# Talking-heads attention and two dense layers in float32: the first stage issued in the order of a list scheduler inside the kernel

## Chip, cores and metric

One core of a Trainium2 chip. The metric is device time in microseconds (us) of one execution, lower is better. Engines by the profile's names: PE (TensorE, matmuls), ACT (ScalarE), DVE (VectorE), POOL (GpSimd), SP (SyncE, which here only issues DMAs).

## What is computed

```python
scores = scale * np.matmul(q, k.transpose(0, 1, 3, 2))      # 4 batches, 12 heads, 448 x 448, head size 64
scores = np.einsum('bhij,hg->bgij', scores, w_pre)          # mix the heads
attn = np.exp(scores - np.max(scores, axis=-1, keepdims=True))
attn = attn / (np.sum(attn, axis=-1, keepdims=True) + 1e-09)
attn = np.einsum('bhij,hg->bgij', attn, w_post)             # mix the heads again
x = np.matmul(attn, v)                                      # as 1792 tokens x 768
x = ((x @ w1) * (x @ w2)) @ w3 @ w_out                      # 768 -> 1024 -> 1024 -> 768
out = np.maximum(np.maximum(x @ v1, x @ v2), x @ v3) @ vo   # 768 -> 768 -> 768
```

The dense weights arrive as 64-bit floats and are turned into float32 on the chip.

## The kernel before

It has two stages. In the first, the attention of all four batches runs with the dense layers of batches 0 and 1 beside it. In the second (`last_two`), the dense layers of batches 2 and 3 run together with seven instead of eight block products. The change leaves the second stage as it is.

**Attention.** A batch has 23 steps (`NP`) of 20 queries, 92 in all. *Scores* (`scores`, L208): a unit of 128 queries of a head pair (or the last 64 of two pairs) is four 64x64 matmuls at L215, one eviction (L217 or L219) and one store to `sdram`; 21 units a batch. *Regroup* (L229) loads the 20 queries back with queries and heads in the partitions, two steps ahead (`AHEAD`). *Mix and softmax* (`mix_softmax`): four matmuls at L250 into the bank pair `m`, the maximum on DVE (L252), two exponentials on ACT (L256), then the weights `kwr` on DVE. *Post* (`post_mix`), one step later: 32 small matmuls at L284 into `p`, copied to `a` on ACT (L291). After every sixth step and the last of a batch, `attend` multiplies by `v` (48 matmuls at L316), and the result goes to `xdram`. The tags `m`, `p` and `s` have one pair of PSUM banks each. A float32 matmul shows as two instructions in the trace.

**Dense work beside it.** All dense products are split in a high and a low half, three matmuls each (`products`, L120). `fuse` forms w3 @ w_out (384 matmuls of 384 columns), `moe(b)` the layers of a batch (864 of 448 columns). A weight block of first use goes through `from_f64` (POOL issues the load `wraw`, one ACT pass, four DVE passes), is split (ACT, then DVE at L164) and stored to `kept`; batch 1 reads it from there. `weight_sums` has POOL form the sums for the second stage.

**What sets the order.** The loop over steps writes a step as regroup, scores, mix, post, and then `fill`s in dense groups of six matmuls at a rate of 2.4 or 3.9 groups a step:

```python
        rate = 2.4 if s < LAG + NP else 3.9
        for third in range(3):
            fill(rate / 6)
            if third:
                some_scores(third)
            fill(rate / 6)
```

The scores of batch b+1 are spread over the steps of batch b, head pair by head pair (`ahead_scores`). The framework then orders the instructions of each engine itself from the program so written; each engine takes its own in that fixed order.

Of the kernel before, what the change touches and what calls it, by code (L numbers as in the profile page):

```python
# [17 lines left out]
P = 128  # L18
# [33 lines left out]
def units():  # L52

    for pr in range(0, HP, 2):
        for x in (pr, pr + 1):
            for it in range(S // P):
                yield [(x, P * it), (x, P * it + HB)]
        yield [(pr, S // P * P), (pr + 1, S // P * P)]
# [3 lines left out]
def attention_talking_heads_moe_kernel(  # L62
# [37 lines left out]
    def from_f64(t, src, w):  # L100
        raw = pa.tile([P, PW], I64, tag="wraw", name="wraw", bufs=3)
        nc.gpsimd.dma_start(raw[:, :w], src)
        words = raw[:, :w].bitcast(U32).rearrange("p (x two) -> p x two", two=2)
        low, high = words[:, :, 0], words[:, :, 1]
        ti = t.bitcast(U32)
        nc.scalar.activation(t, high.bitcast(F32), AF.Abs)  # L106
        nc.vector.tensor_scalar(t, t, F64_MIN, F64_MAX, op0=ALU.max, op1=ALU.min)
        nc.vector.tensor_scalar(ti, ti, 5, 2, op0=ALU.logical_shift_left, op1=ALU.logical_shift_right)
        nc.vector.scalar_tensor_tensor(ti, low, 29, ti, op0=ALU.logical_shift_right, op1=ALU.bitwise_or)  # L109
        nc.vector.scalar_tensor_tensor(ti, high, 0xC0000000, ti, op0=ALU.bitwise_and, op1=ALU.bitwise_or)  # L110

    def wc():
        return pa.tile([P, PW], F32, tag="wc", name="wc", bufs=3)

# [12 lines left out]

# [8 lines left out]
    stored = set()  # L138

    def split_f64(hi, lo, src, w):  # L140
        t = wc()[:, :w]
        from_f64(t, src, w)
        nc.scalar.copy(hi, t)
        nc.gpsimd.tensor_sub(lo, t, hi.bitcast(F32))

    def slab_tiles():
        hi = wp.tile([P, KH * P], F32R, tag="whi", name="whi")
        lo = wp.tile([P, KH * P], F32R, tag="wlo", name="wlo")
        return hi, lo

    def slab(nk, key):
        hi, lo = slab_tiles()
        hi, lo = hi[:, :nk * P], lo[:, :nk * P]
        if key in source and key not in stored:
            t = wc()
            from_f64(t, source[key], PW)
            nc.scalar.copy(hi, t)
            nc.scalar.dma_start(kept[key], t)
            stored.add(key)
        else:  # L160
            t = lo.bitcast(F32)
            nc.sync.dma_start(t, kept[key])
            nc.scalar.copy(hi, t)  # L163
        nc.vector.tensor_sub(lo, t, hi.bitcast(F32))  # L164
        return hi.rearrange("p (k f) -> p k f", f=P), lo.rearrange("p (k f) -> p k f", f=P)

    kp = const.tile([P, HB], F32, name="kp")
    kw = const.tile([P, H, GB], F32, name="kw")  # L170

# [19 lines left out]
    xst, est, ast, vst = {}, {}, {}, {}  # L191

    def load_heads():

        t = [big.tile([P, HP, S], F32, tag=x, name=n) for x, n in (("xhi", "kall"), ("xlo", "qall"))]
        for a, z in ((0, 2), (2, HP)):
            for dst, src, w in zip(t, (kT, qT), (S, P)):
                nc.sync.dma_start(dst[:, a:z, :w], src[0, a:z, :, :w].rearrange("x p j -> p x j"))
        nc.sync.dma_start(t[1][:, :, P:], qT[0, :, :, P:].rearrange("x p j -> p x j"))
        return [[x[:, pr] for x in t] for pr in range(HP)]  # L200

    def load_pair(b, pr):
        t = [pa.tile([P, S], F32, tag=x, name=x, bufs=3) for x in "kq"]
        for dst, src in zip(t, (kT, qT)):
            nc.sync.dma_start(dst, src[b, pr])
        return t

    def scores(b, unit, heads, tag="s", eng=None, out=None):  # L208
        st = out if out is not None else pa.tile([P, 2, S], F32, tag="s", name="s", bufs=2)
        pt = banks(tag)  # L210
        for c, (pr, i) in enumerate(unit):
            k, q = heads[pr]
            for o in range(2):
                sl = slice(o * D, (o + 1) * D)
                nc.tensor.matmul(pt[HB * c:HB * c + HB, o, :S], q[sl, i:i + HB], k[sl], start=True, stop=True)  # L215
        if eng is nc.vector:
            nc.vector.tensor_scalar_mul(st, pt[:, :, :S], D ** -0.5)  # L217
        else:
            nc.scalar.activation(st, pt[:, :, :S], AF.Copy, scale=D ** -0.5)  # L219
        if out is None:  # L220
            issue = nc.sync if eng is nc.vector else nc.scalar
            (pr, i), (other, _) = unit
            if other == pr:
                issue.dma_start(sdram[b][i:i + P, 2 * pr:2 * pr + 2], st)
            else:
                for c, (pr, i) in enumerate(unit):
                    issue.dma_start(sdram[b][i:i + HB, 2 * pr:2 * pr + 2], st[HB * c:HB * c + HB])

    def regroup(b, p):  # L229
        x = pa.tile([P, 2, S], F32, tag="x", name="x", bufs=AHEAD + 1)  # L230
        i = 2 * GI * p
        if i + 2 * GI <= S:
# [625 lines left out]
```

## Time and profile before

| | us |
|---|---|
| median of 3 runs | 1285.13 (1279.38 to 1285.81) |
| the profiled execution | 1290.92 |
| its span, first to last instruction | 1289.0 |
| PE busy | 1151.6 (89%) |
| DVE busy | 743.5 (58%) |
| ACT busy | 599.5 (47%) |
| POOL busy | 211.7 (16%) |
| mean granted TensorE clock | 0.948 of full |
| moved by DMA | 262.56 MB, mean 204 GB/s |

Busy time is the time in which an engine has an instruction under way. A matmul overlaps the next one, so the distance of two starts, and not the length of one, is what a matmul costs. The granted clock has two levels, 2.4 GHz (1.00) and 1.2 GHz (0.50); a mean between them says how the time was shared. All shares of the page are over both stages.

### The profile page before, as it was taken

The page shows a single profiled execution, that of the slowest core. Times are in us where ns is not written, and L with a number is a line of the kernel's source. Part 1 is how long each engine was busy: PE and PEld are TensorE (multiplying, and loading weights), DVE is VectorE, ACT ScalarE, POOL GpSimd, SP SyncE. Part 2 cuts the span into 40 slices and gives each one's busy share as a digit, 9 for nine tenths or more (in the row PEclk, how much of TensorE's full clock was granted, in tenths as well). Part 3 has the DMA queues.
Part 4 walks back from the last instruction along what each step waited for, and adds up shares of the span by engine and source line. Part 5 has one row for each costly group of instructions (what it writes and reads, how often), then busy time and mean ns, then how long its engine had stood idle before and what let it go on. Part 6 is the DMA issues. An engine that isn't in the chain of part 4 may idle for free.

```text
span 1289.0 us, 29211 instructions
## 1 busy us (share of the span) xinstructions
PE 1151.6 (89%) x12348; PEld 923.7 (72%) x12348; DVE 743.5 (58%) x1191; ACT 599.5 (47%) x1139; POOL 211.7 (16%) x245
## 2 busy tenths in 40 slices
PE   5678989997898997887998889989899999999998
PEld 1345757765576875755776677778798889988887
DVE  4764544465764477582654545454377675468784
ACT  3555665555655546563563444345343334333331
POOL 3441211000000000002356645620000000000000
PEclk8789999999998998898898889899999999999999
DMA  9987787775886587766887878662543332133334
GB/s 339 303 256 244 238 259 268 241 243 188 275 263 219 168 267 263 244 226 208 276 292 254 270 242 295 228 189 81 186 129 116 100 118 56 53 99 107 108 97 136
DMA packets 113470, 262.56 MB, mean 204 GB/s; under 512 B 23592, under 2 KB 67644, under 8 KB 113340
## 3 DMA queue, kind: packets, MB, share of 16 engines
q1 hardware_dynamic: 57180, 116.94, 29.9%
q0 software_dynamic: 15456, 77.62, 18.5%
q10 hardware_dynamic: 40704, 66.14, 14.2%
q8 instruction: 97, 1.59, 0.5%
q14 instruction: 33, 0.27, 0.1%
HBM read 176.50 MB, written 84.15 MB: 202 GB/s over the span
## 4 chain that ended last, share of the span: by engine, by line
PE 45%; DMA 16%; DVE 12%; ACT 9%; issue 3%; ACTq 0%; POOL 0%; DVEq 0%; SPq 0%; POOLq 0%
PE w L120 20%; PE p L120 5%; PE m L120 5%; PE s L120 5%; DMA xdram<-xs 3%; PE p L316 3%; PE p L284 3%; DVE wlo L164 2%; ACT e L256 2%; DMA wlo<-kept_w 2%; PE m L250 2%; DVE nmax L252 2%; DVE wc L109 2%; DMA wlo<-kept_m 2%; DMA wlo<-kept_b 1%
## 5 line engine op out<-in xcount | busy, mean ns | idle before, releaser
L256 ACT ACTIVATE e<-m,nmax 128x448 f32<-128x448 f32 (+1 forms) x184 | 114.9, 630 | 128.4 <-DVE nmax L252 104.4
L284 PEld LDWEIGHTS p<-kwr,e 60*64 60x64 f32 x5760 | 116.3, 149 | 76.9 <-issue 33.0
L252 DVE TENSOR_REDUCE nmax<-m 128x2 f32<-128x896 f32 (+1 forms) x92 | 99.8, 1085 | 73.5 <-PE m L250 73.4
L250 PE MATMUL m<-x,kp 60*64 60x448 f32 x720 | 104.8, 606 | 39.3 <-ACT e L256 39.3
L284 PE MATMUL p<-kwr,e 60*64 60x60 f32 x5760 | 119.5, 234 | 17.2 <-DVE kwr L263 13.7
L164 DVE TENSOR_TENSOR wlo<-wlo,whi 128x768 fp32r<-128x768 f32 (+1 forms) x58 | 67.6, 1166 | 112.3 <-ACT whi L163 112.2
L120 PE MATMUL w<-yhi,wlo 128*128 128x448 f32 (+1 forms) x292 | 108.2, 370 | 5.1 <-DVE wlo L164 5.1
L120 PE MATMUL w<-yhi,whi 128*128 128x448 f32 (+1 forms) x292 | 112.7, 386 | 0.0
L120 PE MATMUL w<-hhi,whi 128*128 128x448 f32 (+1 forms) x280 | 107.8, 386 | 5.3 <-ACT hhi L349 5.3
L163 ACT CAST whi<-wlo 128x768 fp32r<-128x768 f32 (+1 forms) x58 | 52.4, 903 | 124.4 <-DMA wlo<-kept_m 42.4
L120 PE MATMUL w<-ylo,whi 128*128 128x448 f32 (+1 forms) x292 | 108.1, 370 | 0.0
L120 PE MATMUL w<-hlo,whi 128*128 128x448 f32 (+1 forms) x280 | 103.6, 370 | 1.3 <-POOL hlo L350 1.3
L120 PE MATMUL w<-hhi,wlo 128*128 128x448 f32 (+1 forms) x280 | 103.1, 368 | 0.0
L215 PE MATMUL s<-k,q 64*64 64x448 f32 x504 | 66.3, 597 | 34.2 <-ACT s L219 34.2
L291 ACT COPY a<-p 128x480 f32<-128x480 f32 x180 | 93.2, 577 | 2.5 <-PE p L284 2.5
L219 ACT ACTIVATE s<-s 128x896 f32<-128x896 f32 x73 | 67.0, 918 | 55.7 <-PE s L215 23.6
L250 PEld LDWEIGHTS m<-x,kp 60*64 60x64 f32 x720 | 26.4, 142 | 82.2 <-ACT e L256 55.9
L316 PE MATMUL p<-a,v 128*64 128x120 f32 (+1 forms) x1536 | 77.3, 260 | 4.8 <-ACT a L291 4.8
L316 PEld LDWEIGHTS p<-a,v 128*64 128x64 f32 x1536 | 73.8, 137 | 10.2 <-ACT a L291 5.8
L106 ACT ACTIVATE wc<-wraw 128x768 f32<-128x768 f32 (+1 forms) x64 | 54.7, 856 | 52.7 <-DVE wlo L164 17.8
L260 DVE TENSOR_SCALAR den<-den 128x2 f32<-128x2 f32 (+1 forms) x92 | 20.8, 226 | 98.1 <-ACT e L256 98.0
L120 PE MATMUL w<-xhi,whi 128*128 128x448 f32 x192 | 75.9, 396 | 0.1
(198 smaller groups left out, 2474.2 us busy)
## 6 DMA issues: line engine op xcount, KB each, us to landing
x<-sdram SPq DMA_DIRECT2D x176, 210.0 KB, 5.5
sdram<-s ACTq DMA_DIRECT2D x62, 448.0 KB, 5.0
wraw<-in_wm POOLq DMA_DIRECT2D x18, 768.0 KB, 6.4
wlo<-kept_m SPq DMA_DIRECT2D x27, 384.0 KB, 3.1
wlo<-kept_w SPq DMA_DIRECT2D x18, 512.0 KB, 3.6
wraw<-in_w3T POOLq DMA_DIRECT2D x16, 512.0 KB, 6.1
kept_m<-wc ACTq DMA_DIRECT2D x18, 384.0 KB, 4.1
wc<-kept_m POOLq DMA_DIRECT2D x18, 384.0 KB, 6.8
```

Of the source, the lines that this page charges most:

```text
L106: nc.scalar.activation(t, high.bitcast(F32), AF.Abs)
L120: nc.tensor.matmul(out, w, r, start=(k == 0), stop=(k == 3 * n_k - 1))
L163: nc.scalar.copy(hi, t)
L164: nc.vector.tensor_sub(lo, t, hi.bitcast(F32))
L215: nc.tensor.matmul(pt[HB * c:HB * c + HB, o, :S], q[sl, i:i + HB], k[sl], start=True, stop=True)
L219: nc.scalar.activation(st, pt[:, :, :S], AF.Copy, scale=D ** -0.5)
L250: nc.tensor.matmul(pt[HB * c:HB * c + HB, u, :S], kp[sl], x[sl, c], start=True, stop=True)
L252: nc.vector.tensor_reduce(out=nmax[:r], in_=pt[:r, :, :S], axis=AX.X, op=ALU.max, negate=True)
L256: nc.scalar.activation(e[:r, u], pt[:r, u, :S], AF.Exp, bias=nmax[:r, u:u + 1], scale=1.0, accum_out=den[:r, u:u + 1])
L284: nc.tensor.matmul(pt[HB * side:HB * side + HB, c, t, :, u * GB:u * GB + m], e[sl, u, j:j + HB], kwr[sl, u, :, :m], start=True, stop=True,)
L291: nc.scalar.copy(ast[b][:, :, :, off:off + w].rearrange("p t g i -> p (t g) i"), pt[:, c, :, :, :w].rearrange("p t g i -> p (t g) i"),)
L316: nc.tensor.matmul(pt[o * D:(o + 1) * D, pr // 3, pr % 3, :], vst[b][:, jc, h * D:(h + 1) * D], a[:, jc, h, :], start=(jc == 0), stop=(jc ...
```

## The change

The first stage is no longer written in the order of its loops. Every piece of work (one unit's four matmuls, one eviction, one DMA, six dense matmuls, ...) is handed to `Plan` with an engine, a duration, a key and the tiles it reads and writes. `Plan.order` then plays the engines through in time: each takes, of what is ready, the piece with the lowest key. A DMA adds its bytes to one pipe at 0.29 MB/us, counts as landed 1.7 us after it has left the pipe, and is offered only while the pipe is less than 2.5 us behind. A piece may name two engines (evictions: ACT or DVE; a weight's low half: DVE or POOL) and goes to the first that is free. `manual_schedule` keeps the instructions in the order in which `emit` writes them.

The keys count steps. `unit` takes scores row by row: K of a whole batch stays in `kall`, Q comes in rows of 128 queries, and the 21 units of batch b+1 have keys one step apart, from 12 steps after batch b's first step on. `fuse` has the keys 6.5 to 23.8, the dense layers of batch 0 24.6 to 62, those of batch 1 from 62 on. Of batch 1, the last product (108 matmuls) is kept for after the attention (`rest_of_one`). The first row of batch 0 is stored in two parts, 40 queries of each head pair first, and the first regroups wait for that part only. `attend` is cut in two halves. Stores that ACT issued are issued by SP.

```diff
+ENGINES = ("PE", "ACT", "DVE", "POOL", "SP")
+HOP = 0.12
+SWITCH = 0.28
+LAND = 1.7
+RATE = 0.29
+FIRST = 2 * 2 * GI
+BACK = 2.5
...
+    def __call__(self, eng, took, key, do, reads=(), writes=(), bytes=0, mode=None):
+        deps = set()
...
+            while loads and pipe - now < BACK:
+                key, x = heapq.heappop(loads)
+                (e, took), = self.ops[x][0].items()
+                if busy[e]:
+                    later.append((key, x))
+                    continue
+                busy[e] = True
+                out.append((x, e, now))
+                pipe = max(pipe, now + took) + self.ops[x][4] / RATE / 1e6
+                heapq.heappush(events, (now + took, 0, x, e))
+                heapq.heappush(events, (pipe + LAND, 1, x, None))
...
+                while not busy[e] and ready[e]:
+                    _, x = heapq.heappop(ready[e])
+                    if taken[x]:
+                        continue
+                    taken[x] = True
+                    took, m = self.ops[x][0][e], self.ops[x][5]
+                    if e == "PE" and m != mode:
+                        took, mode = took + SWITCH, m
+                    busy[e] = True
+                    out.append((x, e, now))
+                    heapq.heappush(events, (now + took, 0, x, e))
+                    heapq.heappush(events, (now + took, 3, x, e))
+                    heapq.heappush(events, (now + took + HOP, 1, x, e))
...
+    def emit(self):
+        for x, e, _ in self.order():
+            self.ops[x][2](e)
...
+    kall = pa.tile([P, HP, S], F32, name="kall", bufs=1)
+    qs = ring(2, [P, HP, P], "q")
...
-    def load_pair(b, pr):
-        t = [pa.tile([P, S], F32, tag=x, name=x, bufs=3) for x in "kq"]
-        for dst, src in zip(t, (kT, qT)):
-            nc.sync.dma_start(dst, src[b, pr])
...
-        if out is None:
-            issue = nc.sync if eng is nc.vector else nc.scalar
-            (pr, i), (other, _) = unit
-            if other == pr:
-                issue.dma_start(sdram[b][i:i + P, 2 * pr:2 * pr + 2], st)
...
+        plan({"ACT": 0.95, "DVE": 1.12}, 0, key + 0.05, evict, bank_of, [where])
+        if whole and not r and not b:
+            for x, (i, z) in enumerate(((0, FIRST), (FIRST, P))):
+                dma("SP", key + 0.06 + 0.8 * x, sdram[b][i:z, 2 * u:2 * u + 2], out[i:z], 3584 * (z - i), [where],
+                    [("sd", b, r - 1 if x == 0 else r, u)])
+        elif whole:
+            dma("SP", key + 0.06, sdram[b][P * r:P * r + P, 2 * u:2 * u + 2], out, 458e3, [where], [("sd", b, r, u)])
...
+        if b == 0 and i < P:
+            rows = [r for r in (-1, 0, 1) if (0, FIRST, P)[r + 1] < i + 2 * GI and i < (FIRST, P, 2 * P)[r + 1]]
+        reads = [("sd", b, r, pr) for r in rows for pr in range(HP)]
...
+        plan("PE", 0.76, key + 0.01, mix, [("x", xn, 0), ("x", xn, 1)], m_bank, mode="q")
+        plan("DVE", 1.1, key + 0.01, lambda _: nc.vector.tensor_reduce(
+            out=nmax[:r], in_=pm[:r, :, :S], axis=AX.X, op=ALU.max, negate=True), m_bank, [("nmax", n)])
...
+            plan({"ACT": 0.58, "DVE": 0.68}, 0, key + 0.03, lambda e, c=c, n=n, off=off: copy(
+                e, a[:, :, :, off:off + n].rearrange("p t g i -> p (t g) i"),
...
+        dma("POOL", key - 0.8, raws[n][:, :w], src, 1024 * w, (), raw)
+        plan("ACT", 0.88 * f, key, lambda _: nc.scalar.activation(t, high.bitcast(F32), AF.Abs), raw, wc)
...
+                dma("SP", key - 1.0, kept[name], t, 393e3, [wc], [("kept", name)])
+                plan("ACT", 0.92, key - 1.0, lambda _: nc.scalar.copy(hi, t), [wc], h)
+                plan(dict(BOTH), 0, key - 0.9, lambda e: ENG[e].tensor_sub(lo, t, hi.bitcast(F32)), [wc] + h, l)
...
+    KEPT = len(DENSE) - KX
...
-    def some_scores(third):
-        if early:
-            scores(0, early.pop(0), first, "s", nc.vector if third == 1 else nc.scalar)
-        elif waiting:
-            scores(*waiting.pop(0))
...
-    for s in range(len(steps) + LAG + 1):
...
-        if s < len(steps):
-            if s + AHEAD < len(steps):
-                regroup(*steps[s + AHEAD])
-            ahead_scores(*steps[s])
-            some_scores(0)
-            mix_softmax(*steps[s])
...
-        rate = 2.4 if s < LAG + NP else 3.9
...
-        for third in range(3):
-            fill(rate / 6)
...
+    TURN = 62.0
+
+    def fuse_at(j):
+        return 6.5 + 17.3 * j / 64
+
+    def first_at(j):
+        return 24.6 + (TURN - 24.6) * j / 144
+
+    def second_at(j):
+        return TURN + (LAST + 1.8 - TURN) * j / 126
...
+        todo = [(0, r, u, (0.5 * u, 3 + u, 8.5 + 0.5 * u)[r - 1])
+                for r in range(1, 4) for u in range(HP if r < 3 else 3)]
+        for b in range(1, B):
+            todo += [(b, r, u, NP * b - 11 + 6 * r + u) for r in range(4) for u in range(HP if r < 3 else 3)]
...
+    streams = [attention_parts(), dense_stream(), summing()]
...
+    with tc.manual_schedule():
+        block_diagonals()
+        plan.emit()
...
+    def rest_of_one():
+
+        ready = [slab(KX, ("o", m)) for m in range(2)]
+        for m in range(KX):
+            hi, lo = ready.pop(0)
+            pt = bank()[:, :S]
```

How this moves the instructions shows at three places. The first is PE at the start of the program; `m`, `p`, `s` are the PSUM bank pairs, `kall` and `q`/`qall` the operands of the scores, `x` a regrouped step, `w` dense work. Before:

```order
L215 MATMUL m<-kall,qall 64x448 x4
...
L215 MATMUL s<-kall,qall 64x448 x4
L120 MATMUL w<-hhi,whi 128x384
L120 MATMUL w<-yhi,whi 128x384
L215 MATMUL s<-kall,qall 64x448 x4
L120 MATMUL w<-hlo,whi 128x384
...
L215 MATMUL s<-kall,qall 64x448 x9
L250 MATMUL m<-x,kp 64x448
```

and now, up to the first `attend`:

```order
L329 MATMUL s<-kall,q 64x448 x16
L389 MATMUL m<-x,kp 64x448 x8
L329 MATMUL s<-kall,q 64x448 x4
L427 MATMUL p<-kwr,e 64x12x5 x32
...
L329 MATMUL s<-kall,q 64x448 x8
L427 MATMUL p<-kwr,e 64x12x5 x32
L389 MATMUL m<-x,kp 64x448 x4
L461 MATMUL p<-a,v 64x120 x24
L565 MATMUL w<-hhi,whi 128x384
```

Dense work stood between the first scores and the first mix; now none comes before the first `attend`, and 72 of its matmuls did before.

The second place is one step of PE beside the dense layers of batch 0. Before, S (L215), mix (L250) and post (L284) stand together between runs of dense rows:

```order
L120 MATMUL w<-xhi,wlo 128x448
L215 MATMUL s<-k,q 64x448 x4
L250 MATMUL m<-x,kp 64x448 x4
L284 MATMUL p<-kwr,e 64x12x5 x32
L120 MATMUL w<-xhi,whi 128x448
```

and now six dense rows stand on either side of the mix (every other row of a run left out):

```order
L329 MATMUL s<-kall,q 64x448 x4
L643 MATMUL w<-xhi,whi 128x448
L643 MATMUL w<-xlo,whi 128x448
L643 MATMUL w<-xhi,wlo 128x448
...
L389 MATMUL m<-x,kp 64x448 x4
L643 MATMUL w<-xhi,whi 128x448
...
L427 MATMUL p<-kwr,e 64x12x5 x32
L643 MATMUL w<-xhi,whi 128x448
```

Up to the last `attend`, PE has 1980 dense matmuls and goes 384 times from one kind of work (64x64 tiles, `attend`, dense) to another; before it had 1920 and 239 times. Behind it stand 132 dense matmuls up to the second stage, before 192.

The third place is SP at the start, where loads and stores are issued. Before:

```order
L302 DMA v<-in_v 128x3x768
L723 DMA sdram_75<-row 128x1792 x3
L303 DMA v<-in_v 64x768
L205 DMA k<-in_kT 128x448
L235 DMA x<-sdram_75 60x2x448 x6
```

and now:

```order
L257 DMA q<-in_qT 128x6x128
L257 DMA sdram_75<-a 40x896
L257 DMA sdram_75<-a 88x896
L257 DMA v<-in_v 128x3x768
L257 DMA sdram_75<-a 40x896 x5
L257 DMA sdram_75<-a 88x896 x5
L257 DMA x<-sdram_75 60x2x448 x4
```

The first `x` waits for stores of 40 queries of each pair in place of whole rows. SP issues 559 transfers in all (386 before), ACT 24 (200 before).

## Rows read from the trace of the kernel before

**Rows 1.** Windows: stretch, PE, PEld, DVE, ACT, POOL busy (count), granted clock, DMA share, GB/s.

```profile
0.00:46.00 46.00, 24.35 (x104) 8.86 (x104) 23.48 (x34) 15.02 (x22) 17.14 (x25) 0.81 0.98 335
46.00:913.00 867.00, 762.18 (x10505) 589.37 (x10506) 474.21 (x768) 453.25 (x909) 194.54 (x220) 0.94 0.73 237
913.00:964.00 51.00, 46.25 (x215) 42.30 (x216) 28.71 (x45) 22.84 (x39) 0.00 (x0) 0.93 0.55 183
964.00:1289.00 325.00, 318.79 (x1527) 283.15 (x1525) 217.12 (x346) 108.42 (x172) 0.00 (x0) 1.00 0.33 98
```

**Rows 2.** Waits of PE, 46 to 913 us: total us, times, longest us.

```profile
PE m L250 <- ACT e L256: 39.3, 22, 5.6
PE s L215 <- ACT s L219: 37.2, 17, 7.4
...
PE w L120 <- DVE wlo L164: 0.8, 2, 0.5
```

**Rows 3.** Timeline of PE around 255 us: start, length, operation, [idle before <- releaser].

```profile
253.16 0.98 PE L215 MATMUL s<-k,q 64*64 64x448 f32 x8 [2.50 <-ACT s L219]
...
261.69 1.77 PE L215 MATMUL s<-k,q 64*64 64x448 f32 x8 [2.85 <-ACT s L219]
```

**Rows 4.** Timeline of PE: one whole step, to the next one's first row.

```profile
269.20 0.98 PE L215 MATMUL s<-k,q 64*64 64x448 f32 x8
270.00 0.93 PE L250 MATMUL m<-x,kp 60*64 60x448 f32 x8
270.75 1.11 PE L284 MATMUL p<-kwr,e 60*64 60x60 f32 x64
271.79 0.47 PE L120 MATMUL w<-xhi,whi 128*128 128x448 f32 x1
...
276.85 0.98 PE L215 MATMUL s<-k,q 64*64 64x448 f32 x8
```

**Rows 5.** Timeline of PE: 18 matmuls of `fuse` and the `attend` behind them.

```profile
152.45 0.44 PE L120 MATMUL w<-hhi,whi 128*128 128x384 f32 x1
152.73 0.34 PE L120 MATMUL w<-hlo,whi 128*128 128x384 f32 x1
...
155.51 0.34 PE L120 MATMUL w<-hhi,wlo 128*128 128x384 f32 x1
155.78 5.14 PE L316 MATMUL p<-a,v 128*64 128x120 f32 x96
```

**Rows 6.** The page's costliest groups: xcount | busy us, mean ns | idle before.

```profile
L256 ACT ACTIVATE e<-m,nmax 128x448 f32<-128x448 f32 (+1 forms) x184 | 114.9, 630 | 128.4 <-DVE nmax L252 104.4
...
L252 DVE TENSOR_REDUCE nmax<-m 128x2 f32<-128x896 f32 (+1 forms) x92 | 99.8, 1085 | 73.5 <-PE m L250 73.4
...
L291 ACT COPY a<-p 128x480 f32<-128x480 f32 x180 | 93.2, 577 | 2.5 <-PE p L284 2.5
...
L316 PE MATMUL p<-a,v 128*64 128x120 f32 (+1 forms) x1536 | 77.3, 260 | 4.8 <-ACT a L291 4.8
```

**Rows 7.** Timeline of PE: the first mix.

```profile
38.17 1.00 PE L250 MATMUL m<-x,kp 60*64 60x448 f32 x1
```

**Rows 8.** Timeline of PE: the first `attend`.

```profile
110.54 5.14 PE L316 MATMUL p<-a,v 128*64 128x120 f32 x96
```

**Rows 9.** DMA view, 0 to 913 us.

```profile
DMA packets 94921, 221.29 MB, mean 242 GB/s; under 512 B 20936, under 2 KB 58588, under 8 KB 94812
```

**Rows 10.** The page's DMA issues: xcount, KB each, median us to landing.

```profile
x<-sdram SPq DMA_DIRECT2D x176, 210.0 KB, 5.5
...
wraw<-in_wm POOLq DMA_DIRECT2D x18, 768.0 KB, 6.4
```

**Rows 11.** Groups view, POOL: low halves of the weights.

```profile
L144 POOL TENSOR_TENSOR wlo<-wc,whi 128x512 fp32r<-128x512 f32 x16 | 20.3, 1272 | 65.3 <-ACT whi L143 60.8 <-issue 4.3
```

**Rows 12.** Timeline of ACT: the last `attend` is evicted.

```profile
912.94 0.66 ACT L323 COPY xs<-p 128x264 f32<-128x264 f32 x2 [1.13 <-PE p L316]
```

**Rows 13.** Timeline of DVE: first difference for the last two batches.

```profile
929.41 0.63 DVE L495 TENSOR_TENSOR t<-t,t 128x448 f32<-128x448 f32 x1 [8.17 <-DMA wlo<-kept_o]
```

More of the change, by code (lines that the diff above doesn't have):

```diff
@@ L137, in attention_talking_heads_moe_kernel @@
                 source[name, m] = src[m]
[L138 to L165, printed above, removed]
+    QK = KX // 2
@@ new lines, in attention_talking_heads_moe_kernel, with turn @@
+    HW = QK * P
+    blocks = [(x, i, KH // 2) for i in range(KH // 2) for x in "ab"]
+    blocks += [(f"m{x}", i, KX // 2) for i in range(KX // 2) for x in range(3)]
+    blocks += [("o", i, KX // 2) for i in range(KX // 2)]
+    sums = {(name, i): dram.tile([P, 4 * HW], F32, name=f"sums_{name}_{i}") for name, i, _ in blocks}
+    ENG = {"ACT": nc.scalar, "DVE": nc.vector, "POOL": nc.gpsimd, "SP": nc.sync}
+    plan = Plan()
+    used = {}
+    def turn(ring, n):
+        used[ring] = used.get(ring, -1) + 1
+        return used[ring] % n
@@ new lines, in dma, with copy, ring @@
+    def dma(eng, key, out, src, nbytes, reads=(), writes=()):
+        plan(
+            eng, 0.55 if eng == "POOL" else 0.42, key,
+            lambda e: ENG[e].dma_start(out() if callable(out) else out, src() if callable(src) else src),
+            reads, writes, bytes=nbytes,
+        )
+    def copy(e, out, src):
+        (nc.scalar.copy if e == "ACT" else ENG[e].tensor_copy)(out, src)
+    def ring(n, shape, tag, dtype=F32, pool=pa):
+        return [pool.tile(shape, dtype, tag=tag, name=tag, bufs=n) for _ in range(n)]
@@ L172, in block_diagonals @@
+    xs = ring(2, [P, 3 * CG * GI], "xs")
+    raws = ring(3, [P, PW], "wraw", I64)
+    wcs = ring(3, [P, PW], "wc")
+    ts = ring(3, [P, S], "t", pool=tmp)
+    slabs = [slab_tiles() for _ in range(3)]
+    pm, pp, pz = (banks(x) for x in "mps")
+    pw = [bank() for _ in range(2)]
+    nc.vector.memset(vt[S % P:, S // P], 0.0)
     def block_diagonals():
@@ new lines, in dense_stream, with summing @@
+    def dense_stream():
+        yield from fuse_parts()
+        yield from dense_parts(0, DENSE, first_at)
+        yield from dense_parts(1, DENSE[:KEPT], second_at)
+    def summing():
+        yield TURN + 0.9
+        yield from sum_parts(sums_at)
+    streams = [attention_parts(), dense_stream(), summing()]
+    heads = [(-20.0 + x, x) for x in range(3)]
+    heapq.heapify(heads)
+    while heads:
+        _, x = heapq.heappop(heads)
+        key = next(streams[x], None)
+        if key is not None:
+            heapq.heappush(heads, (key, x))
@@ L803, in attention_talking_heads_moe_kernel @@
     tail["groups"] = all_groups()
[L804 to L806 removed]
+    behind.append(attention_operands(X))
+    for _ in rest_of_one():
         step()
[L808 removed]
     flush()
```

737 lines of the change are left out of this document (432 added, 305 removed).

## Prediction

> **What bounds the kernel now.** I read the windows first [rows 1]. The second stage, from 964 us on, has PE busy for 318.8 of 325 us at the full clock; the change does not touch it. The 913 us of the first stage are another matter: from 46 to 913 PE is busy for 762 of 867 us, so 105 us are idle, and the granted clock is 0.94, so about 52 us more ((1 - 0.94) x 867) go to the lower level. DVE and ACT are busy for about half of it, DMA has a share of 0.73. No engine is full there: PE has the most work and stands waiting.
>
> For what, the waits tell [rows 2]: 39.3 us for the exponentials of the step before (the mix wants the banks `m` back) and 37.2 us for a score eviction (the next unit wants `s`). That is 76.5 of the 105 us. The timeline shows such waits [rows 3]: the score unit at 253.16 follows 2.50 us of idle time and runs 0.98 us; the one at 261.69, after another, takes 1.77 us, the length at the lower clock. So a wait costs twice: the idle time, and matmuls at 1.2 GHz afterwards. In the PE queue S, mix and post stand side by side, so that nothing is left to do while ACT frees a bank.
>
> **PE's own work, from rows at the full clock.** In one clean step [rows 4] the starts lie apart: scores 0.80 us (269.20 to 270.00), mix 0.75, post 1.04, and 24 dense matmuls 5.06. The run of `fuse` [rows 5] gives 0.174 us a matmul (16 in the 2.78 us from 152.73 to 155.51), but 0.28 after the first and 0.27 before the next kind: about 0.10 us for each change of kind. So a dense matmul of 448 columns is (5.06 - 0.20) / 24 = 0.2025 us. All `attend`s take 77.3 us [rows 6]. Up to the last `attend`:
>
> - both kernels: 84 score units 67, 90 whole mixes 68, 90 posts 94, attend 77, 384 of `fuse` 67: 373 us;
> - before: 1536 dense x 0.2025 = 311, 239 changes of kind = 24: **708 us**;
> - now: 1596 dense x 0.2025 = 323, 384 changes = 38: **734 us**.
>
> The finer mixture costs PE 14.5 us and the dense work that is moved ahead 12. Before, the first stage takes 913 us for 708, so 205 are lost. The change is about those.
>
> **The start.** The first mix starts at 38.17 [rows 7] and the first `attend` at 110.54 [rows 8]; with 20 units, 7 mixes, 6 posts and 72 matmuls of `fuse` PE has done 44 us of work by then, so 66 of the 205 are lost here. Now nothing of `fuse` stands there, and the first regroup waits for 0.86 MB of scores and not for 2.75. Two bounds for the new first `attend`: the transfers ahead of it (K 1.4, Q 0.8, V 1.4, two rows and five units of scores 7.8, ten steps of `x` 4.3, the first weights 2.6) are 18.3 MB, at 335 GB/s and a share of 0.98 [rows 1] 53 us; the chain gives a mix at about 25 us (loads, six units over two evicting engines, store and load), then seven steps of mix 0.75, maximum 1.09 and two exponentials of 0.63 [rows 6] with about a microsecond of hand-overs and some of it at the lower clock, 4.5 us each: 57. I take 58. PE has done 24 us of work by then, so 34 are lost: a gain of 32.
>
> A rule speaks against such small pieces. The Trainium skill (DMA: Bandwidth & Descriptors, Bandwidth) says to batch transfers to 1 MiB for three quarters of the peak and gives 138 GB/s for 64 KB and 341 for 1 MB. By it, at an estimated 240 GB/s for the 140 to 400 KB pieces here, the start would take 76 us and the end would come 18 us later. The measurement speaks against it: the rate above was reached at a share of 0.98, so with many pieces under way at once, those of `x` of 210 KB [rows 10] among them.
>
> **The steps after it.** Of the other 139 lost microseconds, the part of the two waits is 76.5 / 105, 73%, and I let the low clock go with its waits: 101 vanish, 38 stay. Each unit is now evicted by whichever of ACT and DVE is free, and dense matmuls (six take 1.2 us) stand between S and mix and between mix and post. What is late next? Bounds for new waits, which the trace can't show: none, or one for one, 101. I take 15, half of the 28.5 us that PE waits for other things in the same stretch (105 - 76.5), as those are the nearest rows: the new order is fixed too, and real durations will miss its figures (it has 0.89 us for a post that takes 1.04).
>
> Edits at nothing, and what covers them: half of the 180 copies of `a` [rows 6] may go to DVE, some 0.7 us each by the ratio of its evictions, 60 us in 800 beside the 474 that it has [rows 1]; in return POOL takes 30 of 40 subtractions, 1.9 us each by width [rows 11], beside 195 us. ACT loses 175 issues, SP gains them. SP's cover is thin: all its transfers wait in line, so an `x` held up by PE holds up the stores behind it; with `x` two steps ahead and 5.5 us to land [rows 10] there is room for one step of delay.
>
> So the last `attend` ends at 734 + 34 + 38 + 15 = **821 us** (913 before).
>
> **The end.** Between the stages 51 us [rows 1] held 192 dense matmuls; now 132, 12 us less: 39. The other chain there hardly gives more room: from the last eviction [rows 12] to the first difference [rows 13] 16.5 us, then some 20 operations of 0.54 us and six weight subtractions of about 1, 33 to 37 us. Then 325 as before. Span 821 + 39 + 325 = 1185, with 1.9 around it 1187; the runs' median lies 5.8 under the profiled execution, so **1181 us**.
>
> **The rivals.**
>
> *The waits move* (0.07). Scores and mixes wait no more, but posts, `attend` and dense groups take it over, one for one (101 in place of 15). For it: ACT and DVE have no less work. Against: neither is half busy, and a wait here was caused by the place in the queue. Only the start is gained: 1181 + 86 = 1267.
>
> *DMA becomes the bound beside batch 0's dense layers* (0.15). By bytes 94 MB have to move in those 37 steps (weights read 31.5, stored 16; scores 16; `x` 16; the rest 15), 275 us at the 342 GB/s of a full share, while PE has 316 us of work (864 dense matmuls 175, 37 mixes and posts 67, 34 units 27, `attend` 31, changes of kind 16): a share of 0.87, where the stage has shown 0.73 [rows 1] (221.29 MB up to 913 us [rows 9]). If it holds no more than that, the stretch takes 377 us, 40 more than the 337 that I have (316 and its part of the losses): 1221.
>
> *Little is left over* (0.12). The 38 and the 15 go as well but for ten: 1181 - 43 = 1138.
>
> *Slower: first-use weights come late to a PE that can't pass them by* (0.07). Before, PE waited 0.8 us for a low half in that whole stretch [rows 2], as dense work stood behind the attention of a step. Now a dense group stands in front of each mix; if its weights aren't there, the attention behind it stands too. The plan gives a 768 KB load 0.55 + 2.7 + 1.7 = 5 us, the trace 6.4 [rows 10], and seven passes over the block follow. There are 56 such blocks. A delay counts about twice through the clock, and I let half of them fall where PE stands anyway: 56 us for each microsecond of delay a block. From 1.9 us on the gain of 104 us is gone; at 2.2 the time is 1181 + 123 = 1304. Against: loads are offered over two steps, some 17 us, ahead.
>
> **How the numbers follow.** The forecast has 0.56 (1150 to 1215: new waits of 0 to 45, start 53 to 62). The range leaves out half of the first rival and of the best case, the slower one, and the 0.03 for no change: **1135 to 1255**. About 0.5% can be told from no change; the forecast and three of the rivals are faster by more: 0.90; within 0.03; slower 0.07.
>
> **What would show it.** Right: a first `attend` before 65 us; PE's waits for `e` at the mix and for the evictions at the scores under 25 us together; a granted clock of 0.97 or more from 60 to 820; a DMA share near 0.8 there; the second stage as long as before. The DMA rival would show in dense groups waiting for low halves or mixes waiting for `x`, with a share near 0.9 or landing times far over 6 us; the moved waits in `kwr`, `a` and `xs` as releasers; the slower one in PE's waits for `wlo` and `whi`, some 50 of them. The forecast is wrong if the last `attend` ends after 880 or before 770.

## The result, and the profile after

| | before | after |
|---|---|---|
| median | 1284.0 us | **1209.6 us** (1205.8 to 1217.4, 4 runs) |
| ratio | 1 | 0.943, 95% interval 0.938 to 0.949 |
| profiled execution, span | 1290.9, 1289.0 | 1209.3, 1207.5 |
| first `attend` starts | 110.5 | 71.4 |
| last `attend` ends | 913 | 845 |
| second stage starts | 964 | 880.5 |

The changed kernel is 74 us faster, inside the range of 1135 to 1255, but 28.6 above the forecast of 1181. Windows of the changed kernel (stretch, then PE, PEld, DVE, ACT, POOL busy with counts, granted clock, DMA share, GB/s), to be read against [rows 1]:

```profile
0.00:34.00 34.00, 14.12 (x73) 3.59 (x74) 5.54 (x12) 7.95 (x10) 6.65 (x14) 0.71 0.85 287
34.00:71.00 37.00, 24.19 (x496) 12.22 (x494) 27.82 (x48) 18.21 (x41) 4.90 (x6) 0.78 0.79 247
71.00:100.00 29.00, 20.18 (x353) 16.30 (x350) 26.54 (x34) 17.56 (x37) 13.27 (x15) 0.85 0.75 243
...
120.00:340.00 220.00, 205.97 (x2895) 156.42 (x2895) 170.79 (x265) 114.89 (x227) 55.46 (x54) 0.98 0.84 271
340.00:440.00 100.00, 100.00 (x1327) 72.32 (x1324) 68.44 (x111) 52.12 (x98) 13.05 (x12) 1.00 0.70 228
440.00:540.00 100.00, 99.32 (x1366) 73.37 (x1360) 91.85 (x133) 59.42 (x107) 31.18 (x26) 1.00 0.97 312
...
849.00:881.00 32.00, 26.35 (x118) 23.67 (x117) 21.18 (x34) 16.20 (x29) 0.00 (x0) 0.89 0.62 214
881.00:1208.00 327.00, 320.65 (x1545) 286.43 (x1543) 219.29 (x349) 111.28 (x176) 0.00 (x0) 1.00 0.33 99
```

From 340 to 440 PE is busy to the microsecond at the full clock, and from 440 to 540 it is busy for 99.32 of 100 us at a DMA share of 0.97. Most of the losses lie at the start, up to 100 us, where the granted clock is low (0.71 to 0.85) and, from 71 on, DVE is nearly full (26.54 of 29). From 120 to 340 PE is idle for another 14 us. PE's waits from 71 to 849 us (total, times, longest) answer to [rows 2]:

```profile
PE p L427 <- DVE kwr L403: 8.2, 2, 8.0
PE m L389 <- ACT e L396: 5.9, 6, 2.4
PE p L461 <- DVE a L262: 3.4, 2, 2.7
...
PE w L643 <- DVE wlo L620: 0.8, 1, 0.8
PE w L643 <- ACT whi L619: 0.8, 1, 0.8
```

The 39.3 us for `e` have become 5.9, the 37.2 for score evictions none, and low and high halves of the weights of the dense layers are hardly waited for (1.6 us). The 8.0 us for `kwr` are one wait, at 96 us. The start, in PE's timeline (start, length, operation, [idle before <- releaser]), answers to [rows 7, 8]:

```profile
33.63 2.45 PE L389 MATMUL m<-x,kp 60*64 60x448 f32 x8 [9.24 <-DMA x<-sdram]
...
67.97 1.98 PE L427 MATMUL p<-kwr,e 60*64 60x60 f32 x64 [3.79 <-DVE kwr L403]
...
71.38 3.27 PE L461 MATMUL p<-a,v 128*64 128x120 f32 x48
```

And one trip from dense work to a score unit and back, to be read beside [rows 4]:

```profile
450.94 0.36 PE L643 MATMUL w<-ylo,whi 128*128 128x448 f32 x1
451.14 0.36 PE L643 MATMUL w<-yhi,wlo 128*128 128x448 f32 x1
451.43 0.98 PE L329 MATMUL s<-kall,q 64*64 64x448 f32 x8
452.34 0.47 PE L643 MATMUL w<-yhi,whi 128*128 128x448 f32 x1
452.65 0.36 PE L643 MATMUL w<-ylo,whi 128*128 128x448 f32 x1
```

The last dense matmul takes 0.29 us instead of 0.20, the unit 0.91 instead of 0.80, the first dense matmul 0.31: the trip from dense work and back costs some 0.30 us, where two changes of kind at 0.10 had been forecast.

**Where the time went.** From PE's timeline I add up the distances of starts between the first and the last `attend` and sort them: idle time, as the profile gives it; work at the prediction's prices plus `attend` as it ran; what stands over these prices where dense work begins and ends (a trip is one run of other work between dense work); the rest, taken here as lower clock. In us, for some of the experiments of the next section too:

| | before | after | e4 | e8 | e7 | e9 | e10 |
|---|---|---|---|---|---|---|---|
| first `attend` | 110.5 | 71.4 | 70.2 | 71.2 | 70.2 | 83.5 | 70.4 |
| last `attend` starts | 909.1 | 842.9 | 840.3 | 835.5 | 824.0 | 834.0 | 804.7 |
| priced work | 638 | 675 | 676 | 674 | 673 | 669 | 671 |
| trips | 94 | 187 | 125 | 117 | 80 | 99 | 82 |
| their cost | 40 | 57 | 36 | 34 | 22 | 26 | 21 |
| PE idle | 87 | 30 | 44 | 38 | 43 | 42 | 31 |
| rest | 34 | 10 | 14 | 19 | 16 | 13 | 12 |

Before against after: 57 us of waits and 24 of low clock are gone, 17 us of trips and 37 of work are added; 20 of these 37 lay ahead of the first `attend` before. By the first `attend` the changed kernel has lost 47 us, the kernel before 66.

### The profile page after: what moved, and what is told of

It reads as the page before. It is cut to its first block, busy times and chain, and to the rows that moved or that the text cites. A ratio compares the mean times of both kernels' runs of the same rounds, so it can differ in the third digit from the quotient of the medians.

```text
span 1207.5 us, 29292 instructions
## 1 busy us (share of the span) xinstructions
PE 1133.3 (94%) x12348; PEld 888.4 (74%) x12348; DVE 829.7 (69%) x1283; ACT 545.8 (45%) x1017; POOL 267.4 (22%) x275
## 4 chain that ended last, share of the span: by engine, by line
PE 69%; DVE 10%; DMA 7%; ACT 2%; issue 2%; DVEq 0%; POOL 0%; SPq 0%; ACTq 0%; POOLq 0%
PE w L643 24%; PE w L206 9%; PE m L206 6%; PE p L206 6%; PE s L206 6%; PE p L461 5%; PE p L427 5%; PE m L389 4%; PE s L329 3%; DMA wlo<-kept_b 2%; PE w L565 2%; DVE wc L491 2%; DVE wc L493 2%; DVE wc L489 1%; DMA wraw<-in_w3T 1%
## 5 line engine op out<-in xcount | busy, mean ns | idle before, releaser
L329 PE MATMUL s<-kall,q 64*64 64x448 f32 x640 | 84.8, 602 | 7.2 <-ACT s L344 5.7
L613 POOL TENSOR_TENSOR wlo<-wc,whi 128x768 fp32r<-128x768 f32 x30 | 58.6, 1952 | 133.8 <-ACT whi L612 123.1
L643 PE MATMUL w<-yhi,whi 128*128 128x448 f32 x216 | 84.6, 392 | 0.0
L262 ACT COPY a<-p 128x480 f32<-128x480 f32 (+1 forms) x92 | 51.5, 572 | 61.8 <-PE p L427 45.0
L643 PE MATMUL w<-yhi,wlo 128*128 128x448 f32 x216 | 79.3, 367 | 0.0
L643 PE MATMUL w<-ylo,whi 128*128 128x448 f32 x216 | 79.0, 366 | 0.0
L643 PE MATMUL w<-xhi,whi 128*128 128x448 f32 x192 | 76.5, 399 | 2.2 <-DVE t L668 1.4
L262 DVE COPY a<-p 128x480 f32<-128x480 f32 x88 | 56.4, 652 | 30.1 <-ACT a L262 18.5
L619 ACT CAST whi<-wlo 128x768 fp32r<-128x768 f32 (+1 forms) x46 | 40.9, 888 | 70.8 <-DMA wlo<-kept_w 20.3
L643 PE MATMUL w<-xhi,wlo 128*128 128x448 f32 x192 | 71.4, 372 | 0.9 <-DVE wlo L620 0.8
L643 PE MATMUL w<-xlo,whi 128*128 128x448 f32 x192 | 71.0, 370 | 0.0
L491 DVE SCALAR_TENSOR_TENSOR wc<-wraw,wc 128x768 uint32<-128x768 uint32 (+1 forms) x64 | 69.5, 1086 | 1.3
```

Source lines behind the costliest of these rows:

```text
L262: (nc.scalar.copy if e == "ACT" else ENG[e].tensor_copy)(out, src)
L329: nc.tensor.matmul(pt[HB * c:HB * c + HB, o, :S], qs[slot][sl, pr, i:i + HB], kall[sl, pr], start=True, stop=True)
L491: plan("DVE", 1.02 * f, key, lambda _: nc.vector.scalar_tensor_tensor(ti, low, 29, ti, op0=ALU.logical_shift_right, op1=ALU.bitwise_or), r ...
L613: plan(dict(BOTH), 0, key - 0.9, lambda e: ENG[e].tensor_sub(lo, t, hi.bitcast(F32)), [wc] + h, l)
L643: nc.tensor.matmul(pw[w][:, :S], u, r, start=(k == 0 and i == 0), stop=(k == nk - 1 and i == 2))
```

## The experiments

Every experiment edits the changed kernel, and the list is planned anew each time; ratios are to the kernel before. Theory A was at first: the late start explains 13 us of the miss, the price of a change of kind 14, and the gain comes from dense work standing between scores, mix and post on PE.

**e1, whole rows stored once.**

```diff
-        if whole and not r and not b:
+        if False:
...
-        if b == 0 and i < P:
+        if False:
```

> The changed kernel, but the first 128 queries of batch 0 are stored whole, as all others are: the first regroup waits for 2.75 MB of scores and not for 0.86. Theory A (the start is carried to the end one for one): the first mix moves from 33.6 us to about 39 (38.2 in the kernel before), the first attend from 71.4 to about 77, and the last attend and the end come some 5.5 us later: 1215. Rival B (the steps from 60 to 120 us are set by the conversions on DVE, which is busy for 26.5 of 29 us there): the first mix is later, the last attend stays within 2 us: 1210.

Measured: 1213.0, ratio 0.944 (0.942 to 0.947), not told apart from the changed kernel. The first mix:

```profile
34.16 2.33 PE L389 MATMUL m<-x,kp 60*64 60x448 f32 x8
```

Half a microsecond later, not five: the 40 queries stored first bring next to nothing to it. The first `attend` is at 81.0, 9.6 later, and the last only 3.6 later: PE did between 5 and 6 us more of other work before the first. The time of the first `attend` alone says little; what counts is the time lost by then, 47 us in the changed kernel and 51 here.

**e2, the rest behind the first x.** The stores of 88 queries and `v` are given the first `x` as an input.

```diff
+                for key, out, t, nbytes, where, sd in held:
+                    dma("SP", key, out, t, nbytes, [where, ("x", xn[0], 0), ("x", xn[0], 1)], [sd])
...
+        load_v(0, 1.0, [("x", n, u) for n in range(2) for u in range(2)])
```

> The changed kernel, but the stores of the other 88 queries of batch 0 (six of 315 KB) and the load of v (1.38 MB) are made to wait for the first x; in the changed kernel they share DMA with it. Together they are 3.3 MB, 10 us at the 316 GB/s seen there. Theory A: the first mix comes about 6 us earlier (28 instead of 33.6), the first attend and the end too, by 4 to 6: 1204. Rival B (DVE's conversions set the pace of steps 4 to 10): first mix at 28, but the first attend and the end move by less than 2: 1209. A third way: the second row of scores is late for x of steps 2 to 5, and the end comes later.

Measured: 1214.7, 0.947 (0.944 to 0.950). The first mix comes 2.6 us earlier:

```profile
29.46 1.77 PE L331 MATMUL s<-kall,q 64*64 64x448 f32 x8 [4.26 <-DVE s L348]
31.01 1.71 PE L394 MATMUL m<-x,kp 60*64 60x448 f32 x8
```

But what stands behind it is late: the third mix starts at 50.1 (44.0 in the changed kernel), the first `attend` at 77.5 and the last, in the profiled execution, at 851.7. The end comes no earlier, rather later, as the third way had it: nothing is won by holding these transfers back.

**e3, one engine evicts.**

```diff
-        plan({"ACT": 0.95, "DVE": 1.12}, 0, key + 0.05, evict, bank_of, [where])
+        plan({"ACT": 0.95}, 0, key + 0.05, evict, bank_of, [where])
```

and so for the copies of `a` and of `attend`.

> The changed kernel, but scores, the copies of a and those of attend are evicted by ACT alone; the list is planned anew with that. Theory A (the waits of before went because dense pieces stand between scores, mix and post): ACT gets some 90 operations of 0.57 to 0.92 us more, 60 us, and is still about half busy; PE's waits for s and e rise from 12 us to about 25: 1220. Rival C (they went because either engine may evict): most of the 76.5 us of waits and the low clock behind them return: 1270 or more.

Measured: 1211.6, 0.945 (0.941 to 0.948): the same. PE's waits at the mix after the first `attend` are

```profile
PE m L389 <- ACT e L396: 7.5, 6, 2.7
```

and none for `s`. The choice between ACT and DVE for evictions and copies, to which the prediction gave a part in the gain, is worth nothing measurable; rival C is out. The choice between DVE and POOL for a weight's low half was left in.

**e4, pieces of 12.**

```diff
-            for y in range(nk // 2):
+            for y in range(0, nk // 2, 2):
...
-                    for k in (2 * y, 2 * y + 1):
+                    for k in range(2 * ys[0], 2 * ys[-1] + 2):
```

> The changed kernel, but the dense work is planned in pieces of 12 matmuls (one of 6 at the end of a six-slice block), not of 6: 266 changes of kind up to the last attend instead of 384. Theory A (a change costs about 0.135 us, not 0.10, worked out from the trace as 52 us over 384): PE's work falls by 16 us; waits grow by no more than 6: 1196 to 1200. By 0.10: 12 less, 1198 to 1204. Rival D (only pieces as small as 6 cover ACT's evictions): waits for s and e grow by 20 or more: 1215 or more.

Measured: 1207.6, 0.940 (0.937 to 0.943), at most a little better than the changed kernel, between theory A and rival D. Trips fell by 62 and their cost by 21 us, idle time and low clock rose by 18: a trip costs 0.3 us, as the rows say, but here nearly all of the saving was paid back.

**e5, everything by key.** `order` is replaced by one sort: the lowest key whose inputs have been issued goes next, on the first engine that it names.

```diff
+        while ready:
+            key, x = heapq.heappop(ready)
+            out.append((x, next(iter(self.ops[x][0])), key))
+            for y in after[x]:
+                left[y] -= 1
+                if not left[y]:
+                    heapq.heappush(ready, (max(key, self.ops[y][1]), y))
```

> The changed kernel, but the list scheduler's clock is taken out: every operation keeps its key and is issued on its engine in the order of the keys as soon as its inputs have been issued, whether or not they would be there by then; where two engines could do it, the first named does (ACT, which cost nothing measurable in the run with one engine). Scores, mix and post stand side by side in each step again, dense pieces behind them in one run, with one unit a step kept: 174 changes of kind fewer than in the changed kernel. Theory A (the gain is from the ready-driven order, which puts dense work where PE would wait): PE's waits for e and s from 71 us to the last attend return to 50 us or more and the low clock with them: 1250 to 1290. Rival E (one unit a step and evenly spread dense pieces are enough; the list adds only changes of kind): 23 us of changes are saved and no waits come: 1190 to 1200.

Measured: 1395.0, 1.085 (1.080 to 1.090), slower than the kernel before and than both expectations. PE stands still from 69 to 109 us; ACT's timeline and the unit that waited:

```profile
73.82 0.51 ACT L481 CAST hhi<-wc 128x384 fp32r<-128x384 f32 x1 [6.33 <-DVE wc L441]
...
82.43 0.51 ACT L481 CAST hhi<-wc 128x384 fp32r<-128x384 f32 x1 [3.33 <-DVE wc L441]
...
105.98 0.63 ACT L344 ACTIVATE e<-m,nmax 128x448 f32<-128x448 f32 x1
...
108.11 0.94 ACT L292 ACTIVATE s<-s 128x896 f32<-128x896 f32 x1
```

```profile
109.10 1.77 PE L277 MATMUL s<-kall,q 64*64 64x448 f32 x8 [39.60 <-ACT s L292]
```

In this stretch six casts of `w_out` in ACT's queue wait for DVE, each for 3 to 6 us, with the exponential and the score eviction behind them. That is no wait for a busy engine: ACT works for 13.8 of these 40 us. All queues were changed at once here, so it does not tell which order matters.

**e6, rows bunched.**

```diff
-            todo += [(b, r, u, NP * b - 11 + 6 * r + u) for r in range(4) for u in range(HP if r < 3 else 3)]
+            todo += [(b, r, u, NP * b - 11 + 6 * r) for r in range(4) for u in range(HP if r < 3 else 3)]
```

and so for batch 0.

> The changed kernel, but all six units of a row of scores get the key of the row's first step, so they are no longer spread over six steps; the list scheduler stays. Theory A (the order by readiness carries it): the list spreads the units by itself, as each needs the banks s and one of two s buffers: 1205 to 1220. Rival F (one unit a step carries it): units wait for their evictions as before, 37 us of waits and the clock with them: 1245 or more.

Measured: 1216.1, 0.945 (0.939 to 0.951): the same within the interval. One unit a step is no separate gain under this scheduler.

**e7, pieces of a whole block.** As e4, with steps of 4.

> The changed kernel with dense pieces as large as a weight block (18 or 24 matmuls, 3.7 to 4.9 us): 174 changes of kind against 384. Pieces of 12 took 14 us of busy time off PE for 118 changes fewer (0.12 us each) and brought 12 us of waits and low clock. Theory A: here 25 us less work, and waits for e, kwr and the evictions of some 30 us more, since a piece now lasts as long as the chain from the maximum to the second exponential: 1208 to 1220. Rival: waits stay under 20 and it is faster: 1195 to 1203.

Measured: 1191.6, 0.927 (0.923 to 0.932), 1.7% better than the changed kernel and below both expectations. 35 us of trips went for 19 us of idle time and low clock; `attend` took 4 us less. Much of that idle time lies at two places, from 71 to 118 us, where DVE is nearly full, and around 250, with the longest wait

```profile
256.42 1.77 PE L389 MATMUL m<-x,kp 60*64 60x448 f32 x8 [5.99 <-ACT e L396]
```

Here `fuse` is done and no dense layer has begun.

**e8, stay with the kind.** `STAY` is 0.3 steps.

```diff
+                        at = min(range(len(ready[e])), key=lambda y: (
+                            ready[e][y][0] + STAY * (self.ops[ready[e][y][1]][5] != mode), ready[e][y][1]))
```

> The changed kernel, but the list scheduler prefers work of the kind that PE is at: among the ready operations it counts 0.3 steps onto the key of one of another kind. Pieces stay at 6 matmuls; changes of kind (attend counted as a kind of its own) fall from 444 to 300. Theory A (a change costs 0.12 to 0.135 us and is not needed where another piece of the kind is ready): 17 to 19 us less work, waits up by less than 6, as no piece is longer than before: 1193 to 1200. Rival (each change saved is paid for with a wait, as with pieces of 12): 1205 to 1212.

Measured: 1201.2, 0.934 (0.930 to 0.938). Just above theory A's range: trips cost 23 us less, but idle time and low clock are 17 more, where waits were to grow by less than 6.

**e9, PE alone by key.** `queue` is PE's work in the order of e5's sort.

```diff
+                    if e == "PE":
+                        if (self.ops[queue[-1]][1], queue[-1]) not in ready[e]:
+                            break
+                        x = queue.pop()
```

> The changed kernel, but PE alone takes its operations in the order of their keys, whether or not they would be ready; ACT, DVE, POOL and the transfers keep the order by readiness, planned against that PE order. The run with key order on every engine took 1395, with waits of up to 40 us for s and for x behind ACT's and SP's queues, so it did not tell which queue's order mattered. Theory A (PE's choice among ready work carries the gain): waits for s, e and kwr of 50 us and more and the low clock behind them: 1240 or more, as the kernel before or near it. Rival H (the order on ACT, DVE and the transfers carries it, and on PE one run of dense pieces a step is as good): 90 trips into dense work and back fewer at 0.30 us, 27 us less work, and waits within 15 us of the changed kernel's: 1190 to 1200.

Measured: 1200.3, 0.929 (0.926 to 0.933), just above rival H's range. Theory A falls. Scores, mix and post stand side by side on PE as before, and in the timeline nothing waits:

```profile
356.85 0.37 PE L674 MATMUL w<-xhi,wlo 128*128 128x448 f32 x1
357.15 0.98 PE L360 MATMUL s<-kall,q 64*64 64x448 f32 x8
357.95 0.93 PE L420 MATMUL m<-x,kp 60*64 60x448 f32 x8
358.70 1.11 PE L458 MATMUL p<-kwr,e 60*64 60x60 f32 x64
359.74 0.47 PE L674 MATMUL w<-hhi,whi 128*128 128x448 f32 x1
```

Waits of the whole stretch from the first `attend` to the last; `e` and `s` make 4.7 us together, where the kernel before had 76.5:

```profile
PE w L674 <- ACT xhi L617: 10.7, 1, 10.7
...
PE s L360 <- ACT s L375: 3.2, 1, 3.2
...
PE m L420 <- ACT e L427: 1.5, 2, 0.9
```

PE's finer mixture is not the gain but a cost. The new theory, J: the order on ACT and DVE, and perhaps that of the transfers, carries the gain.

**e11 and e12, the two halves of e5.** e11 holds PE, ACT and DVE to the order of the keys in the manner of e9; e12 holds only the transfers to it.

```diff
+                    if e in ("PE", "ACT", "DVE"):
+                        at = queue[e][-1]
+                        if (self.ops[at][1], at) not in ready[e]:
+                            break
```

```diff
+                at = queue["load"][-1]
+                if (self.ops[at][1], at) not in loads or busy[next(iter(self.ops[at][0]))]:
+                    break
+                x = queue["load"].pop()
```

> The changed kernel, with PE, ACT and DVE taking their operations in the order of the keys; POOL and all transfers keep the order by readiness, planned against that. With PE alone so it took 1200, with everything so 1395. Theory J (an operation that waits in ACT's or DVE's queue holds up the evictions, exponentials and maxima behind it, and PE with them; in the run with everything by key, ACT's casts of w_out waited 31.5 us for DVE in eight waits while PE stood for 39.6): most of the 195 us between the two runs return: 1330 or more. Rival K (SP's one line of transfers did it, where it waited 447 us for score evictions): 1195 to 1230.

> The changed kernel, with all transfers taken in the order of their keys, so that one whose data isn't there holds up all behind it in the plan; PE, ACT, DVE and POOL keep the order by readiness, planned against that. Theory J (the engines' queues carry it): the keys of the transfers run ahead of the work by a step or more, so the line seldom stands: 1205 to 1235. Rival K (the line of transfers carries it): most of the 195 us return: 1330 or more.

Measured: e11 1361.0, 1.061 (1.055 to 1.066); e12 1281.5, 0.997 (0.994 to 1.001). Most of the 195 us between e9 and e5 return with the engines' queues, as theory J has it: 161 beside e9, 60 of them by the first `attend` (143.7 against 83.5). But the transfers by key cost 72 us beside the changed kernel, where J allowed 25, and take back the whole gain. PE's waits in e11,

```profile
PE s L363 <- ACT s L378: 94.0, 20, 40.3
```

and in e12 from 67 to 906 us:

```profile
PE m L420 <- ACT e L427: 14.5, 5, 5.3
PE w L674 <- DVE wlo L651: 13.2, 14, 2.1
PE p L458 <- DVE kwr L434: 11.1, 5, 6.5
PE w L674 <- ACT whi L650: 10.7, 11, 1.5
```

Of these, 24 us in 25 waits are for dense weights, 1.6 in the changed kernel: this is the prediction's slower rival, and it is real when transfers stand in line by these keys. e11 also takes the choice of engine away, as e5 does: that is nothing for evictions (e3), but POOL forms 16 low halves of the weights (`wlo`) and not 43 as in e9, and that part was not tried alone. The keys were made as priorities, not as an order, so e5, e11 and e12 show what the readiness rule does with these keys, and not that every order by hand loses as much.

**e10, blocks and a later fuse.**

```diff
-            key = fuse_at(0) - 3.0 + 0.1 * k
+            key = 4.0 + 0.65 * k
...
-        return 6.5 + 17.3 * j / 64
+        return 9.5 + 15.9 * j / 64
```

on top of e7; the first conversion of w3 is moved ahead too.

> The pieces of a whole weight block (1191.6), and the product of the two weights (fuse) planned later and longer: from step 9.5 to 25.4 instead of 6.5 to 23.8, the eight conversions of w_out spread over steps 4 to 8.5 instead of together at 3.5. With whole blocks PE still lost time at two places: 70 to 118 us, where DVE is busy for 25.7 of 29 with those conversions (16 us of waits), and 240 to 262, where no dense work is left between the end of fuse and the first dense layer (10 us of waits, the longest 6.0). Theory A (both are a matter of when dense work is there): the waits of 240 to 262 go, half of those of 70 to 118 stay: 1176 to 1184. Rival I (the early steps go at the pace of their own chain, and the dense work then is missing there): what is gained at 250 is lost before 120: 1188 to 1195.

Measured: 1174.9, 0.910 (0.908 to 0.913): **the fastest version**, 3.5% below the changed kernel by the ratios and just below theory A's range; rival I is out. Its windows at the two places:

```profile
71.00:100.00 29.00, 18.99 (x400) 11.79 (x396) 26.00 (x41) 17.80 (x38) 14.11 (x15) 0.77 0.89 280
...
200.00:300.00 100.00, 93.18 (x1240) 75.68 (x1244) 76.28 (x116) 56.60 (x105) 21.77 (x18) 0.98 0.83 270
```

and those of e7:

```profile
71.00:100.00 29.00, 15.37 (x266) 8.68 (x262) 25.68 (x34) 15.90 (x33) 12.39 (x14) 0.73 0.71 221
...
200.00:300.00 100.00, 85.83 (x1282) 67.33 (x1282) 68.19 (x104) 43.86 (x89) 15.76 (x13) 0.91 0.73 234
```

PE is busy for 3.6 us more in the first and 7.3 in the second, at a higher clock. DVE is as full as it was from 71 to 100 us. Theory A had the size better than the places: from 240 to 262 PE's waits fall from 10.5 to 2.1 us, but from 70 to 118 some 13 of 16 stay.

## Why the prediction was right, and where it was not

**The start: mis-sized.** "A mix at about 25 us" came at 33.6. The first `x` was issued at 22 and took 11.5 us to arrive beside stores and weights (20 to 34 us: 326 GB/s at a share of 0.88); with the other 88 queries and `v` held back (e2) the mix still came at 31.0, so by that run they explain 2.6 of the 8.6 us, and the rest stays open. Seven steps took 5.4 us each ((71.4 - 33.6) / 7) and not 4.5. The first six mixes are 4.9 us apart; the seventh comes 11.8 after the sixth, beside a full DVE (10.52 us of the 11 from 60 to 71). The first `attend` came at 71.4 instead of 58; lost time is 47 us, 34 forecast: 13 of the miss. (For the kernel before, the 44 us of work ahead of the first `attend` belong to the 25 score units of the trace; the 20 in the text would give 40.) That the first regroup waits for fewer bytes gained nothing measurable (e1). The Trainium skill's rule of batching (DMA: Bandwidth & Descriptors, Bandwidth), weighed there, gave 76, which is nearer. The rate behind it is not borne out: from 20 to 34 us those 326 GB/s were reached with such pieces under way, and from 34 to 60 the mean was lower at a lower share (220 GB/s at 0.69). e1, which stores 458 KB at once and not 143 and 315, changed the first mix by half a microsecond; no run here tried pieces of 1 MB.

**Changes of kind: mis-sized.** "About 0.10 us for each", 38 in all, was 57. The part that the prediction had, before and after a run of dense matmuls, came to 39 (20.3 and 18.5). Missing was what score units and mixes pay when dense work and not a mix or post follows, 0.91 us against 0.80 for a unit and 0.75 for a mix: 13 for 85 of them; the other 5 are posts, partly at the lower clock. [rows 4, 5] have no row for it, as S stood before mix and post there; but the unit at 253.16 in [rows 3] has dense work behind it, at 254.07, so the trace of before had the 0.91. The Trainium skill (TensorEngine Tiling (Array Packing), Tiling Modes) says that a change of tiling mode drains TensorE; the trace agrees in so far as a trip from 128x128 to 64x64 tiles and back costs 0.25 to 0.30 us in the changed kernel and its variants (0.43 before, where 15 of the 40 us fall on posts), a price that the section does not give. That the drain is the whole of it is not shown.

**Waits and clock: right in size, a little too dear.** The two waits went (76.5 to 5.9), and "38 stay" plus "15 new" came out as 30 idle and 10 in the rest: 13 better. The granted clock is 0.99 from 71 to 849.

**Their cause: wrong.** The step that failed is "In the PE queue S, mix and post stand side by side, so that nothing is left to do while ACT frees a bank". In e9 they do, and the waits are gone. [rows 3] had the wait; ACT's timeline of the kernel before, to which the prediction did not follow it, has the cause:

```profile
250.97 1.31 ACT L337 CAST xhi<-xlo 128x1344 fp32r<-128x1344 f32 x1 [5.16 <-DMA xlo<-xdram]
252.19 0.91 ACT L219 ACTIVATE s<-s 128x896 f32<-128x896 f32 x1
```

The eviction that PE waited for at 253.16 stood behind a cast that waited 5.16 us for a transfer. ACT was not busy, it was held up by what stood first in its queue. The other wait of [rows 3], at 261.69, has a second form of this: a store in ACT's queue that waited for DVE to finish its data, and the eviction behind it:

```profile
260.28 0.34 ACTq L158 DMA_DIRECT2D kept_a<-wc  x1
260.72 0.92 ACT L219 ACTIVATE s<-s 128x896 f32<-128x896 f32 x1 [2.35 <-DVE kwr L263]
```

Followed back like this through the queues of ACT and DVE, 18 of the 39 waits for `e` and `s` (41.7 of the 76.5 us, the longest among them) lead to a cast or conversion that waited for a load, and 5 (15.5 us) to a store in ACT's queue. Another four, 10 us, lead to an eviction that waited, as far as the semaphores tell, for an earlier store to land; the other 12 are short, 9 us together. That the order of these queues carries the gain is shown for the new keys by e9, e11 and e12. For the kernel before it is read from the trace and not tried: no run put its order back on ACT and DVE, and none put the stores, which the change moved to SP, back on ACT, so what that move alone is worth stays open.

**The sum.** Against the forecast, the start is 13 us longer, trips 19, work 3 and the last `attend` itself 2, while waits and clock are 13 shorter: the last `attend` ends at 845 where 821 stood. Between the stages there are 36 us in place of 39, and the second stage has 327 in place of 325; the runs' median lies at the profiled execution and not 5.8 below it, 6 more. Together that is 28.6. That the time fell into the range owes something to luck: the gain was put down to the wrong queue, and the errors of the terms partly cancel.

**The rivals.** The DMA bound did not show: a share of 0.97 from 440 to 540 with PE busy for 99.3%, so 0.73 was no limit. The waits did not move: those of 71 to 849 us are 30 us in all. The slower rival did not come; e12, where it did, suggests why: by readiness no transfer that could go stands behind one that can't.

## What to carry to other kernels

A wait of PE for an engine that is half busy is a question about that engine's queue: look there for what stood ahead of the late instruction and what that waited for, before moving anything on PE. With these keys, a list by readiness was worth most on the queues of evictions, casts and transfers; on PE, fewer and longer runs of one kind were faster (0.3 us a trip). Filling work must be there in all stretches: e10 gained 17 us over e7 by moving `fuse` and the conversions ahead of it.

## What the runs showed of the hardware that was not expected

A 64x64 score unit costs 0.80 us in front of a mix and 0.91 in front of dense work (and a mix 0.75 in front of a post, 0.91 in front of dense work), so the price of a change depends on both neighbours. DMA held 312 GB/s at a share of 0.97 over 100 us (440 to 540) beside a PE busy for 99% at the full clock.
